# Sums of attention weights added by DMA transfers in the first six pairs, two more pairs masked on VectorE, three weight tiles

## The chip, the cores and the metric

The kernel runs on one core of a Trainium2 chip. The metric is the device time of one execution in microseconds (us). Before the change it is 1156.86 us, the median of three runs (1155.38 to 1157.08). The profiled execution has a span of 1152.4 us, at a mean granted TensorE clock of 0.995.

The engines are named as the profile names them: PE is TensorE's matmul, PEld its weight load, DVE is VectorE, ACT is ScalarE, POOL is GpSimd and SP is SyncE.

## The reference

Two blocks follow each other. The first is attention in which a query sees only the keys of its own hash bucket; the bucket is the sign pattern of six projections:

```python
q_bits = (einsum('bhsd,dk->bhsk', q, proj) > 0);  k_bits = (einsum(... k, proj) > 0)
mask = (sum(q_bits * 2**i))[:, :, :, None] == (sum(k_bits * 2**i))[:, :, None, :]
scores = where(mask, q @ k.T / sqrt(D), -1e9)
attn = exp(scores - max);  attn = attn / (sum(attn, axis=-1) + 1e-09)
x = (attn @ v) -> (B, S, H*D)
```

with 4 batches, 8 heads, 768 positions and a head size of 64. The second block mixes `x` by a Fourier transform over positions and channels, normalises the sum of `x` and the mixed values, and runs an MLP of 512 to 2048 to 512 with a residual:

```python
u = x + real(fft(fft(x, axis=1), axis=2))
out = u + relu(layernorm(u) @ w_ch1) @ w_ch2
```

All is float32; the two weight matrices come in a 64-bit form and are narrowed in the kernel.

## The kernel before

**Pairs of heads.** Attention works on 16 pairs of heads, `n` from 0 to 15, four in each batch: `attention(0)` runs pairs 0 to 3, `attention(1)` pairs 4 to 7, and so on. A pair goes through six steps `c`, one for each 128 keys. In a step, `weigh` (lines 796 to 829) multiplies keys by queries on PE (line 815), takes the exponential on ACT (line 819) into a weight tile `pk` of 128 keys by 2 query halves by 2 heads by 384 queries, and masks it. The tiles `pk` are shared by all pairs in turn; there are `NPK = 2` of them. Each has a 385th column with a small constant, which `values` (line 836) uses on PE when it multiplies the weights by the values.

**Two ways to mask.** For pairs in `LITE` (0 to 4), `prepare` makes sign bits of queries and keys (lines 735 to 742), and line 808 adds a large bias to the scores of pairs that match, by additional matmuls ahead of line 815; the exponential then does the masking. For all other pairs, `prepare` packs the bits into bucket numbers (lines 750 to 778: `bits`, `bt`, `qb`, `kb`), and DVE multiplies the weights by the comparison of bucket numbers, one instruction for each head (line 825). In a LITE pair after pair 0, all copies of transposed queries and keys go to ACT (line 531); in others every second one goes to DVE (line 529).

**The sums.** The denominator is the sum of the weights over all keys. DVE adds the six weight tiles of a pair into `acc` (line 898): the first addition takes tiles 0 and 1, then come four more. In `attention(0)` an addition is cut into two halves, later it is one instruction. At the end of a pair, `scale` (lines 841 to 869) lets PE sum `acc` over partitions by a matmul with ones (line 853), and DVE turns the result into reciprocals and multiplies the pair's output by them (lines 845 to 869).

**The order.** Within the block from line 1393 on, the order of PE, DVE, ACT and POOL is the order in which the program is written (a manual schedule); it covers `attention(0)`. In it, step by step, one slice of the first MLP matrix is narrowed: DVE lines 603 to 612 and ACT lines 611 to 616, while POOL issues the fetch of a later slice (line 657). In the first half of the columns, after every fourth slice PE takes the mean of its columns (line 623) and DVE subtracts it (line 631, centring). Each engine takes its instructions in order. `values` of a step and `scale` of a pair are issued one step later than the weights, so that a pair's sums stand on PE behind the scores of the next pair's step 0. In pair 3, two halves of a `fold` (lines 948 to 966), the first part of the Fourier mix, are put in as well.

From `attention(1)` on, a scheduler orders the work by its own costs; the Fourier mix and the MLP of batch b-1 run interleaved with the attention of batch b, and the second MLP matrix is narrowed during pairs 4 and 5.

Of the kernel before, what the change touches and what calls it, by code (L numbers as in the profile page):

```python
# [11 lines left out]
F32 = mybir.dt.float32  # L12
# [5 lines left out]
ALU = mybir.AluOpType  # L18
AX = mybir.AxisListType

P = 128
B, H, S, D = 4, 8, 768, 64
# [3 lines left out]
NT = S // P  # L26
NPAIR = H // 2
HALF = S // 2
# [451 lines left out]
def _main(  # L480
# [13 lines left out]
    nc = tc.nc  # L494
# [13 lines left out]
    def wt(shape, dtype, tag, name, bufs=2):  # L508
        return work.tile(shape, dtype, tag=tag, name=name, bufs=bufs)
# [4 lines left out]
    def pt(shape, name):  # L514

        turn[0] += 1
        if roomy[0] and turn[0] % 2:
            if turn[0] % 4 == 1:
                return ps_o.tile(shape, F32, tag="o", name=name)
            return ps_sc.tile(shape, F32, tag="sc", name=name)  # L520
        return ps_1.tile(shape, F32, tag="ps", name=name)
# [14 lines left out]
    def load(n, names="qkv", second=nc.sync):  # L536
        b, t = divmod(n, NPAIR)
        for nm in names:
            src = {"q": q, "k": k, "v": v}[nm]
            tag, bufs = ("vn", 2) if nm == "v" else ("qkn", 2)  # L540
            tl = wt([P, NT, 2, D], F32, tag, f"{nm}n{n}", bufs)
            for h in range(2):
                (second if h else nc.sync).dma_start(
                    tl[:, :, h, :], src[b, 2 * t + h].rearrange("(p c) d -> p c d", c=NT)
                )
            nat[nm, n] = tl
# [7 lines left out]
    make_identity(nc, ident)  # L554


    LITE = (0, 1, 2, 3, 4)
    pjw = const.tile([P, P], F32, tag="pjw", name="pjw")
    nc.gpsimd.memset(pjw, 0.0)
    for h in range(2):  # L560
# [8 lines left out]
    pw = const.tile([P, 2, P], BF16, tag="pw", name="pw")  # L569
    ones = const.tile([P, D], F32, tag="ones", name="ones")  # L570
# [3 lines left out]
    norms = const.tile([P, 2, NPAIR * B], F32, tag="norms", name="norms")  # L574


    NPK = 2
    pks = []
    for i in range(NPK):
        pk = const.tile([P, 2, 2, HALF + 1], F32, tag=f"pk{i}", name=f"pk{i}")  # L580
# [39 lines left out]
    def average(f):  # L620
        ps = pt([P, WC], f"wm{f}")
        for c in range(NDC):
            nc.tensor.matmul(
                ps, mean, w1[:, c, f : f + WC], start=(c == 0), stop=(c == NDC - 1)
            )
        return ps
# [68 lines left out]
    def prepare(n):  # L695

        lite = n in LITE
        act = lite and n > 0  # L700
# [89 lines left out]
    @contextmanager  # L790
    def behind():

        with tc.issue_after(last[0].ins), tc.high_priority(offset=AHEAD):
            yield

    def weigh(n, c):
# [3 lines left out]
        heads = [slice(h * D, (h + 1) * D) for h in range(2)]  # L800
        pk = pks[npk[0] % NPK]
        npk[0] += 1
# [28 lines left out]
    def values(n, c, pk, oos):  # L831

        for g in range(2):
            w = HALF + 1 - g
            for h in range(2):
                nc.tensor.matmul(  # L836
                    oos[g][h * D : (h + 1) * D, 0:w], nat["v", n][:, c, h, :],
                    pk[:, g, h, 0:w], start=(c == 0), stop=(c == NT - 1),
                )

    def scale(n, oos, acc):

        x = xs[n // NPAIR][:, n % NPAIR]
        vs = wt([P, 1], F32, "vs", f"vs{n}")
        nc.vector.tensor_copy(vs, oos[0][:, HALF : HALF + 1])
        halves = [x[:, g * HALF : (g + 1) * HALF] for g in range(2)]
        for g, xg in enumerate(halves):
            nc.scalar.activation(xg, oos[g][:, 0:HALF], AF.Identity, bias=vs)
        for g, xg in enumerate(halves):

            ps = pt([P, HALF], f"sum{n}_{g}")
            for h in range(2):
                nc.tensor.matmul(
                    ps[h * D : (h + 1) * D, :], ones, acc[:, g, h],
                    start=True, stop=True,
                )

            rt = wt([P, HALF], F32, "rt", f"rt{n}_{g}", 1)
            nc.vector.transpose(rt, ps)  # L859
            rc = wt([P, HALF // 32], F32, "rc", f"rc{n}_{g}")  # L860
            nc.vector.tensor_scalar(rc, rt[:, 0:HALF:32], S * EPS, None, op0=ALU.add)
            nc.vector.reciprocal(rc, rc)
            rb = wt([P, HALF], F32, "rb", f"rb{n}_{g}", 1)
            nc.vector.tensor_copy(
                rt.rearrange("p (j i) -> p j i", i=32),
                rc[:, :, None].broadcast_to([P, HALF // 32, 32]),
            )
            nc.vector.transpose(rb, rt)
            nc.vector.tensor_tensor(xg, xg, rb, op=ALU.mult)

    def attention(b):
        xs[b] = wt([P, NPAIR, S], F32, "x", f"x{b}")
        pending = []

        def finish():
            n, c, pk, oos, acc = pending.pop(0)
            with behind() if n >= NPAIR and t is not None else nullcontext():
                values(n, c, pk, oos)
            if c == NT - 1:
                scale(n, oos, acc)  # L880

        for t in range(NPAIR):
            n = NPAIR * b + t
            half = fold(b, 0) if t == NPAIR - 1 else iter(())
            if 1 < n + 1 < NPAIR * B:
                load(n + 1)
            ahead = prepare(n + 1) if n + 1 < NPAIR * B else iter(())
            oos = [ps_o.tile([P, 512], F32, tag="o", name=f"oo{n}_{g}") for g in range(2)]
            acc = wt([P, 2, 2, HALF], F32, "t6", f"acc{n}", 2)
            first = None  # L890
            for c in range(NT):
                new = weigh(n, c)
                if c == 0:
                    first = new[:, :, :, 0:HALF]
                else:

                    for g in (0, 1) if b == 0 else (slice(0, 2),):
                        nc.vector.tensor_tensor(  # L898
                            acc[:, g], (first if c == 1 else acc)[:, g],
                            new[:, g, :, 0:HALF], op=ALU.add,  # L900
                        )
                while pending:
                    finish()
                pending.append((n, c, new, oos, acc))
                if c > 2:
                    next(half, None)
                if c > 0:
                    next(ahead, None)
                yield
        t = None  # L910
        while pending:
            finish()
# [25 lines left out]
    def fold(b, cp):  # L938

        x = xs[b]
        if cp == 0:
            zs[b] = wt([P, 2, 2, 2, HALF], F32, "z", f"z{b}", 1)
        for pc in range(2):
            ef = wt([P, 2, S], F32, "t6", f"ef{b}_{cp}_{pc}", 2)
            e = ef[:, 0]
            nc.vector.tensor_tensor(
                e, x[:, cp], x[:, cp + 2], op=ALU.subtract if pc else ALU.add
            )  # L950
            f = ef[:, 1].rearrange("p (r n) -> p r n", r=2)
            for par in range(2):
                nc.vector.tensor_tensor(
                    f[:, par], e[:, 0:HALF], e[:, HALF:S],
                    op=ALU.subtract if par else ALU.add,
                )
            z = zs[b][:, cp, pc]
            n = HALF // 4 - 1
            for at, op in ((0, ALU.add), (2 * n + 3, ALU.subtract)):

                for i, first, last in ((0, 1, n), (n, 2 * n + 2, n + 1)):
                    nc.vector.tensor_tensor(
                        z[:, :, at + i : at + i + last], f[:, :, first : first + last],
                        turned(f, 2 * n + 1 if i == 0 else HALF - 1, last), op=op,
                    )
            nc.vector.tensor_copy(
                z[:, :, 2 * n + 1 : 2 * n + 3], f[:, :, 0 : n + 2 : n + 1]
            )
            yield
# [417 lines left out]
    next(other)  # L1387
    nc.sync.dma_start(ch, cn["ch"].ap())
    nc.sync.dma_start(sq, cn["sq"].ap())


    ET = mybir.EngineType
    with tc.manual_schedule(engines={ET.PE, ET.DVE, ET.Activation, ET.Pool}):
        for _ in prepare(0):
            pass
        roomy[0] = False
        for i, _ in enumerate(attention(0)):
            if i % 5 < 4:
                next(other, None)
        for _ in other:  # L1400
            pass
        pwf = wt([P, 2, P], F32, "t6", "pwf", 2)
        nc.sync.dma_start(pwf, cn["pw"].ap())
        nc.scalar.copy(pw, pwf)
        means = []
        for f in range(DFF // 2, DFF, WC):
            means.append((f, wt([P, WC], F32, "u", f"mean{f}", 2)))
            nc.scalar.copy(means[-1][1], average(f))
    for b in range(B):
# [17 lines left out]
        if b == B - 1:  # L1427
# [6 lines left out]
            ps = pt([1, 3, P], "norms_t")  # L1434
# [65 lines left out]
```

## Time and profile before

| | us | read as |
|---|---|---|
| median of three runs | 1156.86 | the time to beat |
| span of the profiled execution | 1152.4 | first to last instruction |
| PE busy | 1100.6 (96%) | ends of matmuls are modelled |
| DVE busy | 779.9 (68%) | |
| ACT busy | 451.8 (39%) | |
| POOL busy | 74.5 (6%) | issues DMA transfers, few operations |
| DMA moved | 103.11 MB | 89 GB/s over the span |

The page of the profile has the busy shares, the same as tenths in 40 slices of 28.8 us, and groups of like instructions. A row of a group names line, engine, operation, output and inputs with shape, count, the busy time, the mean of one in ns, and after the second bar the idle time of the engine just ahead of these instructions with what ended most of it. A row of a DMA group gives the size of one transfer and the median time from its issue to its landing. The table of windows gives, for a stretch of time, how long each engine was busy in it (with the number of instructions), the granted clock and the mean share of the DMA engines.

In this trace, attention(0) runs from about 12.5 us (the first scores on PE) to 130.6 us; pair 4 ends at 188.5 us and pair 5 at 267 us.

### The profile page before, as it was taken

Reading aid. Unit: us, or ns where it says so; the run is one execution under the profiler, and the core shown is the slowest. Engines: PE = TensorE matmul, PEld = TensorE weight load, DVE = VectorE, ACT = ScalarE, POOL = GpSimd, SP = SyncE. Lnnn points to the kernel's source line nnn. Section 1 sums busy time; section 2 is a strip of 40 time slices with the busy share of each in tenths; the row PEclk is TensorE's granted clock in tenths of the full one; section 3 lists DMA queues with packets and bytes.
Section 4 is the critical chain, followed back from the end, with each engine's and each line's share of the span. In section 5 each row is a group of like instructions: output and inputs, shape, how many; then the busy total and the mean of one; then the engine's idle time right before and its main releaser. Section 6 shows DMA issues by size and latency. Waiting matters only on the chain. (4 is left out here: it accounts for less than half of the span.)

```text
span 1152.4 us, 13749 instructions
## 1 busy us (share of the span) xinstructions
PE 1100.6 (96%) x4921; PEld 641.9 (56%) x4921; DVE 779.9 (68%) x1373; ACT 451.8 (39%) x858; POOL 74.5 (6%) x149
## 2 busy tenths in 40 slices
PE   7989889889999999999999999999999999999996
PEld 4444355444445445644674467654575468768675
DVE  4889959837938455883857877785775877644352
ACT  6778348623222212345224531345424431340420
POOL 1000001100100010020000002002000002010002
PEclk9999999999999999999999999999999999999998
DMA  9534135514611014113042315013104204131401
GB/s 272 151 80 121 40 93 168 167 44 146 224 48 47 17 32 152 28 51 106 15 151 68 86 52 177 15 42 96 47 31 139 64 28 164 48 96 56 154 24 39
DMA packets 131661, 103.11 MB, mean 89 GB/s; under 512 B 81280, under 2 KB 120320, under 8 KB 131584
## 3 DMA queue, kind: packets, MB, share of 16 engines
q1 hardware_dynamic: 123984, 82.35, 24.5%
q0 software_dynamic: 6032, 19.40, 5.1%
q8 instruction: 41, 0.67, 0.2%
q10 hardware_dynamic: 1568, 0.39, 0.2%
q14 instruction: 36, 0.29, 0.1%
HBM read 81.14 MB, written 20.97 MB: 89 GB/s over the span
## 5 line engine op out<-in xcount | busy, mean ns | idle before, releaser
L1214 PE MATMUL o<-w,h 128*128 128x256 f32 x864 | 194.0, 381 | 0.0
L819 ACT ACTIVATE pk<-sc 128x768 f32<-128x768 f32 x192 | 147.8, 808 | 101.2 <-PE sc L815 81.6
L1214 PEld LDWEIGHTS o<-w,h 128*128 128x128 f32 x864 | 162.3, 190 | 30.2 <-issue 3.4
L825 DVE SCALAR_TENSOR_TENSOR pk<-qb,kb,pk 128x768 f32<-128x768 bf16 x132 | 129.3, 1013 | 38.6 <-ACT pk L819 38.5
L815 PE MATMUL sc<-qt,kt 64*128 64x384 f32 x768 | 152.9, 501 | 0.9 <-ACT pk L819 0.9
L836 PE MATMUL oo<-pk,vn 128*64 128x385 f32 (+1 forms) x768 | 149.3, 498 | 1.8 <-DVE pk L825 1.8
L1314 PE MATMUL h_p<-x,w 128*128 128x384 f32 x384 | 140.2, 494 | 2.1 <-ACT qt L531 0.6
L898 DVE TENSOR_TENSOR acc<-acc,pk 128x1536 f32<-128x1536 f32 (+1 forms) x80 | 113.3, 1433 | 9.8 <-ACT pk L819 8.9
L1314 PE MATMUL h_p<-w 128*128 128x384 f32 x288 | 106.3, 492 | 2.9 <-ACT qt L531 1.8
L1314 PEld LDWEIGHTS h_p<-x,w 128*128 128x128 f32 x384 | 69.7, 190 | 56.5 <-ACT h L1346 3.4
L836 PEld LDWEIGHTS oo<-pk,vn 128*64 128x64 f32 x768 | 47.8, 136 | 90.5 <-issue 73.0
L1083 PE MATMUL h<-x,w 128*128 128x384 f32 x256 | 88.6, 499 | 4.1 <-DVE h L1089 3.1
L815 PEld LDWEIGHTS sc<-qt,kt 64*128 64x128 f32 x768 | 66.8, 186 | 44.7 <-issue 23.2
L1065 PE MATMUL o<-w,h 128*128 128x512 f32 x192 | 85.2, 596 | 0.6 <-DVE rt L859 0.6
L1314 PEld LDWEIGHTS h_p<-w 128*128 128x128 f32 x288 | 53.1, 190 | 43.4 <-ACT qt L531 2.4
L1083 PEld LDWEIGHTS h<-x,w 128*128 128x128 f32 x256 | 48.1, 193 | 40.6 <-issue 5.0
L1065 PEld LDWEIGHTS o<-w,h 128*128 128x128 f32 x192 | 35.5, 190 | 43.8 <-issue 41.7
L926 POOL DMA_DIRECT2D out_dram<-w x30 | 16.5, 552 | 468.7 <-issue 426.6
L1226 DVE SCALAR_TENSOR_TENSOR w<-o,rs,w 128x256 f32<-128x256 f32 x42 | 20.1, 481 | 32.2 <-PE o L1214 32.2
L1244 ACT COPY w<-o 128x256 f32<-128x256 f32 x18 | 6.7, 372 | 81.7 <-PE o L1214 81.7
L988 PE MATMUL cs<-ch,z 128*128 128x128 f32 (+3 forms) x192 | 31.8, 316 | 4.7 <-ACT kt L531 2.6
L1214 PE MATMUL o<-w 128*128 128x256 f32 x144 | 34.6, 383 | 1.2 <-DVE u L1226 0.9
(159 smaller groups left out, 1320.3 us busy)
## 6 DMA issues: line engine op xcount, KB each, us to landing
w<-ad SPq DMA_DIRECT2D x168, 128.0 KB, 2.0
w<-bd SPq DMA_DIRECT2D x42, 512.0 KB, 4.4
zraw<-in_moe_w_ch_dram POOLq DMA_DIRECT2D x21, 512.0 KB, 4.1
vn<-in_v_dram SPq DMA_DIRECT2D x32, 192.0 KB, 3.3
qn<-in_q_dram SPq DMA_DIRECT2D x31, 192.0 KB, 3.3
kn<-in_k_dram SPq DMA_DIRECT2D x31, 192.0 KB, 3.3
ad<-st SPq DMA_DIRECT2D x8, 512.0 KB, 3.7
bd<-st SPq DMA_DIRECT2D x8, 512.0 KB, 3.5
```

Of the source, the lines that this page charges most:

```text
L815: last[0] = nc.tensor.matmul(ps[:, h, 0:HALF], kt[rows, ks], qt[rows, qs], start=kb is not None, stop=True,)
L819: nc.scalar.activation(pk[:, g, :, 0:HALF], ps[:, :, 0:HALF], AF.Exp, scale=SCALE)
L825: nc.vector.scalar_tensor_tensor(w, qb[:, h].rearrange("p (g s) -> p g s", g=2), kb[:, h, c : c + 1], w, op0=ALU.is_equal, op1=ALU.mult,)
L836: nc.tensor.matmul(oos[g][h * D : (h + 1) * D, 0:w], nat["v", n][:, c, h, :], pk[:, g, h, 0:w], start=(c == 0), stop=(c == NT - 1),)
L898: nc.vector.tensor_tensor(acc[:, g], (first if c == 1 else acc)[:, g], new[:, g, :, 0:HALF], op=ALU.add,)
L926: nc.gpsimd.dma_start(out[b, s0 : s0 + 2 * w - 1 : 2, cols], src[at : at + w, cols])
L988: nc.tensor.matmul(ps[:, pc + 2 * lo : pc + 2 * hi - 1 : 2], z[:, cp, pc, par, t * P : (t + 1) * P], ch[:, cp, pc, lo:hi], start=(cp == 0) ...
L1065: nc.tensor.matmul(ps, hr, w2[:, fc, cols], start=(i == 0), stop=(i == len(rows) - 1))
L1083: nc.tensor.matmul(ps, w1[:, c, fc * P : (fc + 1) * P], x[:, c, g * HALF : (g + 1) * HALF], start=(c == 0), stop=(c == NDC - 1),)
L1214: nc.tensor.matmul(ps, a[:, r], right7[i][:, r], start=start and r == 0, stop=r == HF // 2 - 1, skip_group_check=not start,)
L1226: nc.vector.scalar_tensor_tensor(t[:, cols], src, r, t[:, cols], op0=ALU.mult, op1=ALU.add)
L1314: nc.tensor.matmul(ps, ring[n % NR][:, k], right[i][:, k], start=start and k == 0, stop=k == 1, skip_group_check=not start,)
```

## The change

In pairs 0 to 5 (`QUEUED`), the additions of steps 2, 3 and 4 leave DVE. Instead POOL issues a DMA transfer that reads a weight tile and adds it to `acc`. The additions of steps 1 and 5 stay on DVE. To make the transfer one run of bytes for each partition, `acc` gets the 385th column too. Pairs 2 and 3 leave `LITE`, so that DVE masks them and PE doesn't. A third weight tile lets a transfer read one tile while the next two are filled. As pair 2 needs the constant `pw` for its bucket numbers, this is loaded and converted early instead of after attention(0).

```diff
-    LITE = (0, 1, 2, 3, 4)
+    LITE = (0, 1, 4)
+
+    QUEUED = range(6)
...
-    NPK = 2
+    NPK = 3
...
-                    ps[h * D : (h + 1) * D, :], ones, acc[:, g, h],
+                    ps[h * D : (h + 1) * D, :], ones, acc[:, g, h, 0:HALF],
...
-            acc = wt([P, 2, 2, HALF], F32, "t6", f"acc{n}", 2)
+            acc = wt([P, 2, 2, HALF + 1], F32, "t6", f"acc{n}", 2)
...
                 if c == 0:
-                    first = new[:, :, :, 0:HALF]
+                    first = new
+                elif n in QUEUED and 1 < c < NT - 1:
+                    nc.gpsimd.dma_start(acc, new, accum_op=ALU.add)
                 else:
...
-                            acc[:, g], (first if c == 1 else acc)[:, g],
-                            new[:, g, :, 0:HALF], op=ALU.add,
+                            acc[:, g], (first if c == 1 else acc)[:, g], new[:, g],
+                            op=ALU.add,
                         )
...
+    pwf = wt([P, 2, P], F32, "u", "pwf", 2)
+    nc.sync.dma_start(pwf, cn["pw"].ap())
...
         for i, _ in enumerate(attention(0)):
+            if i == 0:
+                nc.scalar.copy(pw, pwf)
...
-        pwf = wt([P, 2, P], F32, "t6", "pwf", 2)
-        nc.sync.dma_start(pwf, cn["pw"].ap())
-        nc.scalar.copy(pw, pwf)
```

## The prediction

> **What bounds the kernel now.** The busy shares come first. TensorE (PE) is busy for 1100.6 of 1152.4 us, so a change pays only where PE stands still or loses work. The 40 slices (28.8 us each) tell where that is:
>
> ```profile
> PE   7989889889999999999999999999999999999996
> DVE  4889959837938455883857877785775877644352
> DMA  9534135514611014113042315013104204131401
> ```
>
> From the tenth slice on PE is at 9 nearly throughout; ahead of it lies attention(0), where PE stands at 8 or 9 and VectorE (DVE) too. I cut that stretch by pairs with the table of windows. The bounds are the times at which a pair's sums reach PE (line 853); the four pairs of attention(0) come first, then pairs 4 and 5.
>
> ```profile
> core 0: us, PE busy (x) PEld busy (x) DVE busy (x) ACT busy (x) POOL busy (x), PEclk, DMA share, GB/s
> 12.50:43.90 31.40, 30.46 (x170) 13.80 (x172) 23.30 (x39) 24.44 (x44) 2.62 (x5) 1.00 0.79 249
> 43.90:75.40 31.50, 28.86 (x160) 12.98 (x160) 26.83 (x48) 23.95 (x44) 2.35 (x5) 1.00 0.44 122
> 75.40:101.90 26.50, 25.25 (x151) 11.26 (x152) 25.09 (x45) 23.92 (x44) 0.00 (x0) 1.00 0.33 85
> 101.90:130.60 28.70, 24.08 (x139) 10.48 (x137) 25.42 (x53) 16.74 (x32) 0.11 (x1) 1.00 0.39 97
> 130.60:188.50 57.90, 53.53 (x296) 29.72 (x295) 42.70 (x78) 29.09 (x54) 3.69 (x7) 1.00 0.33 99
> 188.50:267.00 78.50, 70.51 (x263) 35.82 (x262) 50.21 (x84) 38.91 (x73) 4.77 (x9) 0.98 0.32 100
> ```
>
> Pair 0 is PE's (30.46 of 31.40). Pair 2 has two engines full at once: PE 25.25 and DVE 25.09 of 26.50. Whatever takes work from PE there and gives it to DVE makes DVE the bound. Pairs 4 and 5 leave PE 4.4 and 8.0 us of idle time. The groups give the prices:
>
> ```profile
> L825 DVE SCALAR_TENSOR_TENSOR pk<-qb,kb,pk 128x768 f32<-128x768 bf16 x132 | 129.3, 1013 | 38.6 <-ACT pk L819 38.5
> L898 DVE TENSOR_TENSOR acc<-acc,pk 128x1536 f32<-128x1536 f32 (+1 forms) x80 | 113.3, 1433 | 9.8 <-ACT pk L819 8.9
> L808 PE MATMUL sc<-qkb 64*128 64x384 bf16 x120 | 20.8, 327 | 5.5 <-ACT pk L819 5.1
> ...
> zraw<-in_moe_w_ch_dram POOLq DMA_DIRECT2D x21, 512.0 KB, 4.1
> ```
>
> A mask costs 1.01 us; in the timeline of DVE two in a row take 1.94. The second row mixes forms: in attention(0) an addition is two halves, 1.82 us together in the timeline; from pair 4 on it is one of 1.75.
>
> **What the Trainium skill says.** "DMA: Bandwidth & Descriptors", Anatomy of one DMA, prices a transfer issued from GpSimd at 2.0 us plus its bytes over 436 GB/s. That gives 3.2 us for 512 KB; the row above shows 4.1 us, so the price is rather low here. "Collectives: The Full Stack", The bandwidth ceiling, says that a sum in the DMA path is slowed because "the add needs **two source reads**". No addition by DMA is in the trace of before. The DMA page's Rules for kernel authors say that an accumulating transfer must wait for the semaphore of an earlier one on the same bytes; the changed program has these waits, so the three transfers of a pair run one after another.
>
> **The change part by part.**
> Removed from DVE: additions c = 2, 3, 4 of six pairs, 3 x 1.82 = 5.5 us in each of pairs 0 to 3, 3 x 1.75 = 5.3 us in pairs 4 and 5.
> Removed from PE (pairs 2 and 3 leave LITE): in the timeline a masking matmul pair of line 808 delays the next by 0.17 us, 12 x 0.17 = 2.0 us per pair; the bits take 0.8 + 0.5 + 0.2 us (lines 750, 764, 774) instead of 3.1 (line 735), 1.6 less. Together 7.2 us.
> Added to DVE: 12 masks in each of pairs 2 and 3, 6 x 1.94 = 11.6 us per pair. Preparing a masked pair takes 3.0 us (two qt copies 0.8, kt 0.55, bt 0.55, qb 0.95, kb 0.18) against 2.8 for a LITE one. ScalarE (ACT) loses 1.3 us of copies and gets one of 0.8 per pair.
>
> So DVE ends nearly even over attention(0): -22 + 23 + 0.4 us. But its order is written out by hand, and the load moves from pairs 0 and 1 into 2 and 3. From one scale() to the next, DVE's order in the changed program holds:
> - pair 1: scale 5.3, five weight slices of 1.9 (9.5), centring 2.5, preparing 3.0, two additions 3.6, the first mask of pair 2 1.9: 25.8 us.
> - pair 2: scale 5.3, five slices 9.5, six steps of masks 11.6, preparing 3.0, additions 3.6: 33.0 us.
> - pair 3: scale 5.3, one slice 1.9, five steps of masks 9.7, additions 3.6, half a fold 6.4, bits of pair 4 2.8: 29.7 us.
> Before, scale() began at 43.80, 75.74, 101.95 and 129.55 us (line 845 in the timeline). Pairs 2 and 3 together took 53.8 us and now need at least 62.7: **+8.9 us**, with PE waiting. Pair 1 is bound by ACT and PE; its 31.9 us lose 1.6 of PE work, 0.5 of ACT and 1.1 of PE's wait for qkb: 28.9.
>
> The added waits. DVE's addition c = 5 waits for the last transfer of its pair, and behind it on DVE's queue stand weight slices, masks or centring, then scale(); PE's sums wait for that addition, and all of the next pair's matmuls stand behind the sums. One transfer adds 788 KB. Nearest bounds: 3.8 us (the page's price, bytes once), 5.6 us (bytes twice, for two reads), and 9.1 us from the trace alone (128 KB took 2.0, 512 KB 4.1; that slope carried to 1,540 KB). I take 4.7, midway between the first two: the DMA engines' bytes go twice, but reads and writes overlap. Then:
> - pair 0: c = 2 is weighed at 28.6 us. The DMA engines are still full with weights (share 0.79), so 2 us more for the first: 35.3, 40.0, 44.7; addition to 46.5; centring and a slice behind it 4.4: scale(0) at 50.9, **+7.1**.
> - pair 1: c = 2 is ready 9.5 us after scale(0); + 14.1 + 1.8 + 3.8 (slice and mask behind it) = 29.2: 80.1 us.
> - pair 2: c = 2 is masked 15.6 us after; + 14.1 + 1.8 + 3.8 = 35.3: 115.4.
> - pair 3: 12.9 + 14.1 + 1.8 = 28.8, below DVE's own 29.7: 145.1, against 129.55: +15.5 us.
>
> After that, relief: PE's 12.4 us of idle time in pairs 4 and 5 stand partly behind DVE (1.4 us for qt, whose copy on DVE stood behind an addition; single waits for masks) and partly behind weight transfers (DVE waits 3.5 us for zraw). I take half, -6.2. The third weight tile frees ScalarE's exponentials from the last reader but one: at most the 4.9 us that PE waited for pk in attention(0), worth nothing where DVE binds. Loading pw earlier: one 128 KB transfer (2.0 us) and 0.4 us of ACT in pair 0, where ACT has 7 us free: nothing. Columns of 385 instead of 384: nothing. Sum: +15.5 - 6.2 = **+9.3 us, 1166 us**.
>
> **The rivals.**
> 1. The additions are quick (3.8 us): by the same steps 48.2, 77.1, 110.1, 139.8; +10.3 - 6.2: 1161.
> 2. They cost two full reads (5.6 us): 53.6, 85.5, 123.5, 155.0; +25.5 - 6: 1176. At 9.1 us: 64.1, 106.5, 155, 197, or 1218. For: the quoted sentence, and loads that land later than priced. Against: both operands lie in SBUF, not in HBM.
> 3. Faster: transfers hide, pair 1 shrinks to PE's own 26.5 us (scale(3) at 43.8 + 26.5 + 62.7 = 133.0, +3.5), and pairs 4 and 5 give back all 12.4: -8.9, 1148; with two thirds of it 1152. For: the windows show DVE full in 185 to 205 us, so 5.3 us less there may go through whole. Against: pairs 2 and 3 have more DVE work than time.
> 4. The two sides cancel: 1157.
>
> **How the numbers follow.** Transfers between 3.8 and 5.6 us with DVE binding: 0.54 (1161 to 1176, likeliest 1166). Slower transfers: 0.14. Faster: 0.25. No change: 0.07. Slower is thus 0.68. The range from 1148 to 1186 reaches from rival 3 to somewhat beyond 5.6 us; some 0.07 lies below it and 0.12 above.
>
> **What would show it.** After: DVE at 9 throughout pairs 2 and 3, with the distance of scale(1) to scale(3) 62 us or more; DVE waiting at the additions' second group for a DMA, and PE's sums for acc; the adding transfers landing in 4 to 6 us; pairs 4 and 5 shorter. Wrong if the transfers land under 4 us and pairs 0 and 1 shrink, or if scale(3) comes before 134 us.

## The result: 1221.6 us, 5.7% slower, and the profile after

The changed kernel takes 1221.63 us, the median of four runs (1219.56 to 1225.16), against 1156.12 us for the kernel before on the same chip. The ratio is 1.057, with an interval of 1.054 to 1.060. The forecast said slower, but 1166 us, and its range ended at 1186 us: the direction was right and the loss was seven times as large as forecast.

The slices of the changed kernel's page, each 30.6 us long, show where it is lost:

```profile
PE   4876678897999999999999999989999999999996
DVE  1366587395396755489485778779486778545352
PEclk8879799998999999999999999999999999999998
DMA  8754753658064111411304231411303121331501
```

From the eleventh slice on TensorE (PE) is nearly as full as before. In the first eight it is not, and neither is VectorE (DVE), which the forecast wanted to see at 9 throughout pairs 2 and 3 (slices 4 to 7: it shows 6, 5, 8, 7). An engine that has too much work is full; these two wait. The row of the granted clock holds 7 and 8 where it held 9 before.

The windows of the changed kernel run from one scale() to the next; the columns are the stretch, its length, the busy time of the five engines with their instructions, the granted clock, the DMA share and the rate:

```profile
core 0: us, PE busy (x) PEld busy (x) DVE busy (x) ACT busy (x) POOL busy (x), PEclk, DMA share, GB/s
12.50:68.00 55.50, 34.38 (x172) 14.40 (x172) 18.50 (x31) 24.82 (x45) 5.17 (x8) 0.80 0.74 194
68.00:110.90 42.90, 33.86 (x170) 13.81 (x168) 24.28 (x46) 23.80 (x42) 5.23 (x8) 0.86 0.64 145
110.90:155.60 44.70, 29.91 (x136) 11.06 (x134) 31.06 (x52) 23.95 (x42) 2.61 (x3) 0.81 0.52 106
155.60:191.90 36.30, 26.63 (x120) 10.28 (x116) 28.52 (x53) 16.82 (x31) 2.72 (x4) 0.95 0.58 124
191.90:248.40 56.50, 50.29 (x254) 28.49 (x253) 32.96 (x69) 24.78 (x46) 5.27 (x8) 0.91 0.50 121
248.40:332.60 84.20, 74.61 (x288) 38.79 (x288) 49.60 (x89) 41.05 (x78) 8.54 (x14) 0.94 0.49 136
```

scale() begins at 68.0, 110.9, 155.6 and 191.9 us. Against the kernel before it is 24.2, 35.1, 53.6 and 62.4 us late; pairs 4 and 5, from scale() to scale(), add only 3.0 and 2.0 us, so nearly all the loss is in attention(0). In no window is VectorE busy for more than four fifths of the time. VectorE's 31.1 us in pair 2 are close to the 33.0 us that the prediction summed up for it; the stretch lasts 44.7.

What VectorE and TensorE wait for stands in the groups and in the list of DMA issues (three rows of groups: busy time and mean ns, then idle time and its main releaser; one issue row: count, KB, median us to landing):

```profile
L827 DVE SCALAR_TENSOR_TENSOR pk<-qb,kb,pk 128x768 f32<-128x768 bf16 x156 | 152.4, 1013 | 41.0 <-ACT pk L821 41.0
...
L901 DVE TENSOR_TENSOR acc<-acc,pk 128x1540 f32<-128x1540 f32 (+1 forms) x50 | 81.2, 1630 | 31.2 <-DMA acc<-pk 29.9
...
L855 PE MATMUL sum<-acc,ones 128*64 128x384 f32 x128 | 28.8, 551 | 19.9 <-DVE acc L901 18.2
...
acc<-pk POOLq DMA_DIRECT2D x18, 770.0 KB, 6.8
```

The 24 more masks are there at their old price (x156, 1013 ns) and 30 additions are gone (x50). But VectorE idles 29.9 us in front of additions until an adding transfer has landed, and TensorE 18.2 us in front of the sums until that addition is made. A transfer takes 6.8 us (5.7 to 8.4), not 4.7. In the kernel before, the sums waited 2.4 us for additions:

```profile
L853 PE MATMUL sum<-acc,ones 128*64 128x384 f32 x128 | 25.3, 492 | 2.4 <-DVE acc L898 2.4
```

Two more rows come from the list of waits over the first 300 us (total, times, longest):

```profile
ACT qt L531 <- DVE qt L529: 18.4, 5, 6.6
...
ACT pw L1404 <- DMA pwf<-k_pw: 13.6, 1, 13.6
```

In the first row it is the place that is new, not the sum: the same list of the kernel before has

```profile
ACT qt L531 <- DVE qt L529: 21.0, 7, 6.6
```

but after the first few us these waits all lie behind attention(0), from 147.9 us on. Two of the changed kernel's, 4.6 and 6.6 us, lie in pairs 1 and 2.

The second row is a single wait, and the timelines of ScalarE and TensorE show what it does (start, length, and in brackets the idle time before and its releaser):

```profile
29.22 0.41 ACT L1404 CAST pw<-pwf 128x256 bf16<-128x256 f32 x1 [13.58 <-DMA pwf<-k_pw]
```

```profile
32.57 0.50 PE L810 MATMUL sc<-qkb 64*128 64x384 bf16 x2 [13.64 <-ACT pk L821]
32.84 1.51 PE L817 MATMUL sc<-qt,kt 64*128 64x384 f32 x4
```

The narrowing of pw stands in ScalarE's queue in front of the exponentials of step 1. Its load was issued behind ch, sq and the first weight slices, while the DMA engines were nearly full (a share of 0.89 from its issue at 19.6 us to its landing at 29.2). How long loads take there stood in the list of DMA issues of the kernel before:

```profile
sq<-k_sq SPq DMA_DIRECT2D x1, 770.0 KB, 15.8
ch<-k_ch SPq DMA_DIRECT2D x1, 512.0 KB, 13.5
```

For 13.6 us ScalarE does nothing; TensorE stops too, in front of scores that it can't make before ScalarE has taken an exponential. When TensorE starts again, four scoring matmuls take 1.51 us; in pair 0 of the kernel before they took 0.81:

```profile
18.60 0.81 PE L815 MATMUL sc<-qt,kt 64*128 64x384 f32 x4
```

The Trainium skill, "TensorE: Matmul & The Clock Gate", Part 1, says that TensorE's clock falls to half after an idle window of some 3.4 us and comes back after as long at work. The 1.51 us after a wait of 13.64 us agree with that, and so does the end of it: at 38.27 us, 5.7 us after the restart, four scoring matmuls take 0.81 us again.

### The profile page after: what moved, and what is told of

The parts are those of the page before. It is cut to its first block, busy times and chain, and to the rows that moved or that the text cites. A ratio compares the mean times of both kernels' runs of the same rounds, so it can differ in the third digit from the quotient of the medians.

```text
span 1223.4 us, 13688 instructions
## 1 busy us (share of the span) xinstructions
PE 1119.7 (92%) x4893; PEld 647.1 (53%) x4893; DVE 772.7 (63%) x1367; ACT 451.7 (37%) x854; POOL 90.3 (7%) x168
## 2 busy tenths in 40 slices
DMA packets 134253, 117.30 MB, mean 96 GB/s; under 512 B 81568, under 2 KB 120608, under 8 KB 134176
## 5 line engine op out<-in xcount | busy, mean ns | idle before, releaser
L827 DVE SCALAR_TENSOR_TENSOR pk<-qb,kb,pk 128x768 f32<-128x768 bf16 x156 | 152.4, 1013 | 41.0 <-ACT pk L821 41.0
L817 PE MATMUL sc<-qt,kt 64*128 64x384 f32 x768 | 160.3, 528 | 3.6 <-ACT pk L821 2.8
L838 PE MATMUL oo<-pk,vn 128*64 128x385 f32 (+1 forms) x768 | 154.9, 511 | 7.6 <-DVE pk L827 6.5
L901 DVE TENSOR_TENSOR acc<-acc,pk 128x1540 f32<-128x1540 f32 (+1 forms) x50 | 81.2, 1630 | 31.2 <-DMA acc<-pk 29.9
L817 PEld LDWEIGHTS sc<-qt,kt 64*128 64x128 f32 x768 | 70.0, 196 | 58.0 <-issue 27.4
L1317 PEld LDWEIGHTS h_p<-w 128*128 128x128 f32 x288 | 53.3, 190 | 41.9 <-ACT qt L531 2.3
L1068 PEld LDWEIGHTS o<-w,h 128*128 128x128 f32 x192 | 35.5, 190 | 43.8 <-issue 41.7
L855 PE MATMUL sum<-acc,ones 128*64 128x384 f32 x128 | 28.8, 551 | 19.9 <-DVE acc L901 18.2
L850 ACT ACTIVATE x<-oo,vs 128x384 f32<-128x384 f32 x32 | 16.8, 576 | 63.6 <-DVE vs L847 63.0
## 6 DMA issues: line engine op xcount, KB each, us to landing
vn<-in_v_dram SPq DMA_DIRECT2D x32, 192.0 KB, 3.4
qn<-in_q_dram SPq DMA_DIRECT2D x31, 192.0 KB, 3.3
kn<-in_k_dram SPq DMA_DIRECT2D x31, 192.0 KB, 4.5
```

The lines of the kernel that those rows point to most:

```text
L817: last[0] = nc.tensor.matmul(ps[:, h, 0:HALF], kt[rows, ks], qt[rows, qs], start=kb is not None, stop=True,)
L827: nc.vector.scalar_tensor_tensor(w, qb[:, h].rearrange("p (g s) -> p g s", g=2), kb[:, h, c : c + 1], w, op0=ALU.is_equal, op1=ALU.mult,)
L838: nc.tensor.matmul(oos[g][h * D : (h + 1) * D, 0:w], nat["v", n][:, c, h, :], pk[:, g, h, 0:w], start=(c == 0), stop=(c == NT - 1),)
L855: nc.tensor.matmul(ps[h * D : (h + 1) * D, :], ones, acc[:, g, h, 0:HALF], start=True, stop=True,)
L901: nc.vector.tensor_tensor(acc[:, g], (first if c == 1 else acc)[:, g], new[:, g], op=ALU.add,)
L1068: nc.tensor.matmul(ps, hr, w2[:, fc, cols], start=(i == 0), stop=(i == len(rows) - 1))
```

## The experiments

Three explanations were set against each other. Theory A: waits add up, namely the transfers' chain, the wait for pw and the copies of q and k that ScalarE and VectorE share; TensorE's slow clock makes each longer. Rival C: the masks on VectorE carry the loss. Rival D: the transfers cost by crowding the loads of weights. Further rivals come with single runs. Each run is timed beside the kernel before, which took 1154.7 to 1155.5 us.

### Each part alone

**pw later.** The changed kernel with

```diff
-            if i == 0:
+            if i == 3:
                 nc.scalar.copy(pw, pwf)
```

> The changed kernel, with the narrowing of pw on ScalarE moved from step 0 to step 3 of pair 0; the load stays where it is. Theory A (the copy waits 13.58 us for its load at 29.22 us, in ScalarE's queue ahead of the exponentials of step 1, and TensorE cools meanwhile): the 13.6 us come back nearly whole, 1205 to 1210 us; scale(0) at about 54 us instead of 68. Rival B (the sums wait for the adding transfers anyway, which start when the vectors are there, so that the wait for pw is hidden beside them): less than 4 us come back, 1218 to 1222 us. By the prediction, which costed the early load at nothing: 1221 us.

1210.0 us, ratio 1.048 (1.045 to 1.050): 11.6 us come back, which just meets theory A's 1205 to 1210. scale(0) is at 56.3 us, not 54: the narrowing still waited 8.7 us for the load at its new place, and VectorE's last addition waited 9.6 us for a transfer.

**pw early, nothing else.** The kernel before with the load behind sq's and the narrowing after step 0:

```diff
+    pwf = wt([P, 2, P], F32, "u", "pwf", 2)
+    nc.sync.dma_start(pwf, cn["pw"].ap())
...
         for i, _ in enumerate(attention(0)):
+            if i == 0:
+                nc.scalar.copy(pw, pwf)
...
-        pwf = wt([P, 2, P], F32, "t6", "pwf", 2)
-        nc.sync.dma_start(pwf, cn["pw"].ap())
-        nc.scalar.copy(pw, pwf)
```

> The kernel before, with nothing changed but the load and narrowing of pw, which go where the changed kernel has them. Theory A: the same wait of 13 to 14 us in front of the exponentials of step 1, nothing later to hide it: 1169 to 1172 us. Rival B (the wait costs only together with the adding transfers): 1156 to 1160 us.

1169.6 us, ratio 1.012 (1.010 to 1.015): 14.2 us, as theory A has it. The wait measured 15.2 us, and scale(0) came 14.8 us later. A move that the prediction costed at nothing costs more than the whole loss that it forecast.

**The transfers alone.** The changed kernel with pw loaded and narrowed after attention(0), where the kernel before has it, and

```diff
-    LITE = (0, 1, 4)
+    LITE = (0, 1, 2, 3, 4)
```

> The kernel before with the adding transfers, the longer sums and the third weight tile, but with pairs 2 and 3 masked on TensorE and pw loaded late as before. Theory A (three transfers of some 6.8 us in a chain for each pair, and the sums, scale() and the next pair's buffers behind them): each of six pairs loses some 4 to 8 us, 1180 to 1200 us. Rival C (the masks on VectorE carry most of the loss, the transfers only relieve VectorE): 1150 to 1160 us. Rival D (the transfers cost by crowding the loads of w1 and w2): a loss too, but with VectorE waiting for zraw, not for acc.

1194.3 us, ratio 1.034 (1.032 to 1.036), within theory A's numbers, though the six pairs lose from 12.8 us (pair 0) down to 2.5 (pair 5) and not 4 to 8 each. The first four scale() are 12.8, 19.7, 29.5 and 34.3 us late although VectorE has less to do. In the waits over the first 300 us, VectorE stood 48.0 us before additions for transfers and 10.5 us for zraw, where it stood 7.0 us for zraw before. So rival D has a share, but a small one, and rival C's "1150 to 1160" is out. The transfers are felt on ScalarE too: it stood 9.6 us, in pairs 0 and 2, until a transfer had read its weight tile and the tile was free again, three tiles or not.

**The masks alone.** The changed kernel with pw narrowed at step 3 and

```diff
-    QUEUED = range(6)
+    QUEUED = ()
```

> The changed kernel without any adding transfer (all additions on VectorE) and with the narrowing of pw at step 3: what is left of the change are the masks of pairs 2 and 3 on VectorE and the third weight tile. Theory A: what the prediction's sum gave for VectorE in pairs 2 and 3, +8.9 us, and up to 6 us for copies of q and k that wait behind it: 1163 to 1172 us. Rival C: 1190 us or more. Rival E (the third tile and the lighter TensorE pay for it): 1150 to 1157 us.

1194.7 us, ratio 1.034 (1.032 to 1.036). Theory A's figure missed by over 20 us, and rival C's "1190 us or more" came true: the masks alone cost as much as the transfers alone, so neither carries the loss by itself. Theory A's figure failed for two reasons. It took over the prediction's +8.9 us, which had the additions c = 2, 3, 4 gone from VectorE; here they are back, 5.5 us in each pair. The prediction's sums then become 38.5 us for pair 2 and 35.2 for pair 3; the trace gives 41.9 and 36.2, where the kernel before took 26.2 and 27.6. And scale(0) was 5.9 us late, from a wait of 4.9 us that was left for pw. Here VectorE is the fullest engine in pairs 2 and 3, busy for 36.4 of 41.9 and 34.1 of 36.2 us. The two halves, +38.9 and +39.3 us alone, give +54.6 together (the run with pw later): the transfers do take load off VectorE, as they are meant to, but for more than it is worth.

The trace of this run also shows the third wait, in pair 1 on ScalarE's timeline:

```profile
59.58 0.69 ACT L531 COPY qt<-trq 128x192 f32<-128x192 f32 x2 [5.03 <-DVE qt L529]
```

With LITE, ScalarE makes all four copies of qt itself; in pair 1 of the kernel before it made them without a wait:

```profile
48.52 1.21 ACT L531 COPY qt<-trq 128x192 f32<-128x192 f32 x4
```

Without LITE the copies alternate, and VectorE's stand behind scale(), a weight slice and an addition. ScalarE waits in order, with step 1's exponentials behind it.

### What makes a transfer slow

**Plain copies.** The kernel with the transfers alone, and

```diff
-                    nc.gpsimd.dma_start(acc, new, accum_op=ALU.add)
+                    nc.gpsimd.dma_start(acc, new)
...
-                        nc.vector.tensor_tensor(
-                            acc[:, g], (first if c == 1 else acc)[:, g], new[:, g],
-                            op=ALU.add,
+                        nc.vector.scalar_tensor_tensor(
+                            acc[:, g], (first if c == 1 else acc)[:, g], 1.0, new[:, g],
+                            op0=ALU.max, op1=ALU.add,
                         )
```

> The kernel with the adding transfers alone (pairs 2 and 3 masked on TensorE, pw late), but the 18 transfers copy the weights into acc instead of adding them; VectorE's additions become max-with-1-then-add of the same size. Left out: the sums over c = 2, 3, 4. Theory A (a transfer takes 7.0 us because it adds: acc is read as well as written): a plain copy of 770 KB lands in 4 to 5 us, each of the four first pairs gets some 4 to 6 us back, 1168 to 1182 us. Rival F (770 KB from memory on the chip to memory on the chip take that long in any case, or queue behind loads): 6 to 7 us a copy, 1188 to 1196 us.

This kernel leaves out the sums over three of the six steps. 1160.2 us, ratio 1.004 (1.003 to 1.005), below even theory A's range: 34 us of the 39 are gone. Bytes (117.30 MB in both), queue, chain and waits on semaphores are the same, and VectorE's other form of addition takes as long as the old one (mean 1629 ns against 1630); only the addition in the transfer is gone, and GpSimd's issue takes 0.53 us instead of 0.87. The issue row of this run:

```profile
acc<-pk POOLq DMA_DIRECT2D x18, 770.0 KB, 4.4
```

4.4 us against 7.0 with addition. What crosses the pairs' limit is the chain of three: three medians make 13.2 us, which fit almost beside the work of three steps (VectorE still stands 22.6 us for transfers, 12.3 of them in pair 0), and 21.0, which do not (48.0).

**Half the bytes.** The changed kernel with pw narrowed in pair 1, and

```diff
-                    nc.gpsimd.dma_start(acc, new, accum_op=ALU.add)
+                    nc.gpsimd.dma_start(acc[:, 0], new[:, 0], accum_op=ALU.add)
+                    nc.vector.tensor_tensor(
+                        acc[:, 1], acc[:, 1], new[:, 1], op=ALU.add
+                    )
```

> The changed kernel with pw narrowed in pair 1, and only the first half of the rows (acc[:, 0], 385 KB) added by the transfers; VectorE adds the second half in three more additions of 0.95 us for each pair. Theory A (the time of an adding transfer goes with its bytes, and the chain of three is what the pairs wait for): a transfer takes 3.5 to 5 us, the waits for acc at the last addition nearly go, VectorE has 2.9 us more in each pair: 1180 to 1198 us against 1212 with whole transfers. Rival H (a fixed cost for each adding transfer): still 6 us or more, with more work on VectorE, 1212 us or more.

1190.3 us, ratio 1.031 (1.029 to 1.033), against 1212.0 with whole transfers. In its list of DMA issues:

```profile
acc<-pk POOLq DMA_DIRECT2D x18, 385.0 KB, 4.3
```

Half the bytes take 2.5 us less, so rival H, a fixed cost, is out. It is no way out: VectorE takes the other half back.

**With and without other loads.** These medians mix two things, and the traces of the runs above and below part them. An addition beside which no other transfer is in flight takes 5.7 us (at 223.6 us in the changed kernel; the quickest of each run with whole additions takes as long), half of it 3.9 us (at 152.4 us in the run with half the bytes), and a plain copy 3.5 us (at 192.0 us in the run with masks and plain copies, below). The windows of the first and the last, with the columns as above:

```profile
223.60:229.30 5.70, 4.67 (x30) 2.61 (x30) 2.29 (x4) 3.11 (x6) 0.87 (x1) 1.00 0.70 138
192.00:195.50 3.50, 3.50 (x26) 2.42 (x25) 1.14 (x2) 1.22 (x3) 0.53 (x1) 1.00 0.55 225
```

Length times DMA share, an estimate of the work of the DMA engines, gives 4.0 us for the addition and 1.9 us for the copy: twice as much for the same 770 KB. So a lone addition is at the 5.6 us that the prediction had for two full reads. The 1.1 us more of the median go with other loads: the slowest addition of the changed kernel, 8.4 us at 81.9 us, has loads of q, k and weights in flight beside it.

### pw, relief and the third tile

**pw in pair 1.** The changed kernel with `if i == 6` in place of `if i == 0`:

> The changed kernel with the narrowing of pw in pair 1 (step 0), when its load has long landed: what the change costs without any wait for pw. With the narrowing at step 3 of pair 0 it still waited 4.9 us or so for the load. Theory A (waits add up): another 4 to 6 us less than there, 1203 to 1207 us, and scale(0) to scale(3) near 50, 93, 138 and 173 us; the prediction's own steps with 6.8 us in place of 4.7 for a transfer give 57, 93, 134 and 169. Rival B (hidden beside the transfers): 1209 to 1211 us.

1212.0 us, ratio 1.048 (1.046 to 1.051). Theory A missed, and the time is next to rival B's 1209 to 1211: no gain over step 3. ScalarE no longer waits for pw, but scale(0) stays at 56.6 us. VectorE's timeline says why:

```profile
50.61 1.83 DVE L901 TENSOR_TENSOR acc<-acc,pk 128x770 f32<-128x770 f32 x2 [17.75 <-DMA acc<-pk]
```

Without the wait for pw, pair 0 ends at its transfers, which share the DMA engines with the first loads (6.7 to 11.6 us each). The run with the transfers alone has the same scale(0), 56.6 us. So pw costs 14.2 us in the kernel before and 9.6 us here.

**Transfers in pairs 4 and 5 alone, and the third tile alone.** The transfers' kernel with `QUEUED = (4, 5)`:

> The kernel before with a third weight tile, the longer sums and adding transfers in pairs 4 and 5 alone. The prediction's step (relief of VectorE in these pairs gives back 6.2 us of TensorE's idle time): about 1150 us. Theory A (no relief: what VectorE saves is lost again to zraw loads that stand behind the transfers on GpSimd, and to the wait for the last transfer; with the adding transfers in all six pairs these two lost 3.8 and 2.5 us): 1157 to 1164 us.

The kernel before with `NPK = 3`:

> The kernel before with a third weight tile and nothing else of the change. The prediction (nothing in pairs 0 to 3 waits for a weight tile, some TensorE and ScalarE waits in pairs 4 and 5 might go): 1150 to 1157 us. Rival G (the third tile moves other tiles in the memory or lets the exponentials run ahead in front of more urgent work): 1158 us or more.

The third tile alone gives 1151.1 us, ratio 0.996 (0.995 to 0.998): a small gain. The waits of TensorE for pk at line 808 (total, times, longest, in the kernel before)

```profile
PE sc L808 <- ACT pk L819: 5.1, 9, 1.2
```

fall to 3.1 us in 7 waits in it. With the transfers in pairs 4 and 5 as well it is 1154.1 us, ratio 0.999 (0.998 to 1.000). Both expectations for that run left the tile out; beside the tile alone, the transfers there cost 3 us. There is no relief: TensorE stands idle for 5.3 and 10.0 us in pairs 4 and 5, and for 4.3 and 8.6 us with the tile alone. Zraw's loads, behind the transfers on GpSimd, take 5.2 us where the tile alone has 4.0.

### What the shared copies cost

**Copies on ScalarE, adding transfers.** The changed kernel with pw narrowed in pair 1, and

```diff
-        act = lite and n > 0
+        act = n in (1, 2, 3, 4)
```

> The changed kernel with pw narrowed in pair 1, and with all copies of the turned q and k for pairs 1 to 4 on ScalarE, where the changed kernel shares those of pairs 2 and 3 with VectorE. ScalarE waits 6.6 us for VectorE's copy in pair 2 and some 4.6 in pair 1. Theory A (these late copies hold up the exponentials): about the sum of these waits less the copies' own 2 us for each pair, 1203 to 1208 us. Rival I (the pairs end at the adding transfers or at VectorE's work anyway): 1210 to 1214 us.

1203.8 us, ratio 1.042 (1.041 to 1.044), against 1212.0: 8.2 us, as theory A has it.

**Masks with plain copies.** The changed kernel with pw narrowed in pair 1 and the plain copies as above:

> The changed kernel with pw narrowed in pair 1 and with plain copies (4.4 us in the run with the transfers alone) in place of the adding transfers (6.9 us), VectorE's additions again as max-with-1-then-add. Left out: the sums over c = 2, 3, 4. It is the prediction's case: a transfer of about the 4.7 us that was assumed, no wait for pw. The prediction's steps without the relief of 6.2 us that did not come: 1172 us, less the 4.4 us that the third tile brings, 1168 us, with scale(0) to scale(3) at 50.9, 80.1, 115.4 and 145.1 us. Theory A (these steps hold, late copies on top): 1166 to 1178 us. Rival J (the prediction also had the cost of the masks on VectorE too low): 1183 us or more, with scale(2) later than 122 us.

The same sums are left out. 1182.2 us, ratio 1.023 (1.021 to 1.025), between theory A and rival J, whose other sign, scale(2) later than 122 us, is there. Copies took 4.0 us; scale() came at 51.1, 87.9, 125.3 and 156.7 us. Pair 0 is right to 0.2 us. Pair 1 takes 36.7 us where the prediction's steps have 29.2, and most of the miss arises there.

**The same with the copies on ScalarE:**

> As the run with masks and plain copies (1182.2 us; the sums over c = 2, 3, 4 again left out), with the copies of the turned q and k for pairs 1 to 4 on ScalarE alone. Theory A (the 10 us that the prediction's steps miss there are the shared copies that stand behind other work on VectorE): 1172 to 1176 us, with the distance from scale(0) to scale(1) back from 36.7 us to some 30 to 32. Rival J (the masks cost VectorE more than the prediction has): 1179 to 1183 us.

Here too the sums are left out. 1175.2 us, ratio 1.017 (1.016 to 1.019): 7.0 of the 10 us, mostly theory A's, and rival J's 1179 to 1183 is out, though pair 1 still takes 33.5 us and not 30 to 32. The windows of pairs 1 and 2, first with plain copies and the copies of q and k shared:

```profile
51.12:87.85 36.73, 31.11 (x170) 13.19 (x168) 23.98 (x45) 24.13 (x43) 4.02 (x8) 0.92 0.55 169
87.85:125.33 37.48, 27.79 (x134) 10.59 (x134) 31.07 (x51) 24.00 (x42) 1.58 (x3) 0.86 0.40 122
```

and with those copies on ScalarE:

```profile
51.66:85.17 33.51, 29.59 (x170) 12.57 (x168) 23.08 (x43) 24.79 (x46) 4.22 (x8) 0.97 0.61 185
85.17:119.34 34.17, 26.86 (x134) 10.81 (x134) 29.95 (x48) 24.65 (x45) 1.58 (x3) 0.90 0.46 138
```

Both stretches are 3.3 us shorter with the same TensorE instructions (x170, x134). TensorE's busy time falls by 1.5 and 0.9 us with the clock's rise from 0.92 and 0.86 to 0.97 and 0.90. Pair 3, whose clock falls from 0.94 to 0.90, takes 1.4 us longer; pairs 4 and 5 are some 2 us shorter together.

**Tile and copies on the kernel before**, `NPK = 3` and `act = 0 < n < 7`:

> The kernel before with a third weight tile (which alone gave 1151.1 us) and the copies for pairs 5 and 6 on ScalarE alone as well. ScalarE waits 18 to 21 us over pairs 4 to 7 for VectorE's copies of qt. If these waits reach TensorE, whose idle time in pairs 4 and 5 is 12.4 us: 1145 to 1149 us; if TensorE has other work ready: 1150 to 1152 us.

1150.5 us, ratio 0.996 (0.995 to 0.998), the same as the tile alone: in pairs 4 and 5 the waits for shared copies do not reach TensorE, as it was expected for the case that it has other work ready. These two versions are faster than both kernels, by 0.4% against the one before.

## Why the prediction was wrong, point by point

The runs form a ledger from the forecast to the measurement. Its last three lines are each the difference of two measured kernels; the rest line is what is left, with the third tile's gain of 4.4 us in it. The sizes hold for this order: without masks the additions cost 34 us more than copies, with them 29.8; pw costs 14.2 us in the kernel before and 9.6 here. The rest is seen in the traces: by scale(3) the kernel of 1175.2 us is 7.0 us behind the prediction's steps, 4.3 of them in pair 1 and 3.0 in pair 3.

| step | us | time after it |
|---|---|---|
| forecast | | 1166 |
| "relief −6.2" did not come | +6.2 | 1172 |
| rest, not parted by a run | +3.0 | 1175.2 |
| copies shared by ScalarE and VectorE | +7.0 | 1182.2 |
| transfers that add, instead of copies | +29.8 | 1212.0 |
| wait for pw in front of pair 0's exponentials | +9.6 | 1221.6 |

- **"I take 4.7, midway between the first two."** This is the term that failed most. The adding transfer took 6.8 us; a plain copy took 4.0 to 4.4. "Reads and writes overlap" was the reason for going below two full reads, and no run supports it: even a lone addition takes 5.7 us, at the bound of 5.6. What inside the transfer doubles the work no run shows. The second half of the error is that other loads were priced for the first transfer of pair 0 alone, with 2 us; that one took 11.6 us (pw narrowed in pair 1). The prediction's own steps with 6.8 us in place of 4.7 give 57, 93, 134 and 169 us for the first four scale(), 24 us more at the last. Without the wait for pw the trace shows 56.6, 99.8, 145.0 and 181.6, and with the copies of q and k on ScalarE as well 56.6, 96.9, 139.2 and 174.8. So the chain's mechanism was right. What is left there is in pair 1, 40.2 us for 35.5: its first transfer is issued 1.6 us after its weights, behind a weight fetch in GpSimd's queue, and takes 9.4 us beside that fetch and the loads of q and k.
- **The row for 9.1 us, "or 1218".** That it comes near 1221.6 us is luck: no transfer takes 9.1 us in the median, and the wait for pw and the copies made up the difference. The slope that is named there gives 9.7 us besides, not 9.1.
- **"Loading pw earlier … nothing."** A term that was put at nothing costs 9.6 us. The cost was looked for in the wrong place: the load is 2.0 us and ScalarE has 7 us free, but the narrowing is in ScalarE's in-order queue before the load can land. Its issue stood behind slices of 512 KB, ch and sq, and the trace of before already had 13.5 and 15.8 us for the last two. The prediction asked what is queued behind the added waits on VectorE, and not behind this one on ScalarE.
- **"Pair 1 is bound by ACT and PE; its 31.9 us lose …: 28.9."** It counted which copies go from ScalarE to VectorE and not the order: ScalarE's own qt copy waits 4.6 us in pair 1 and 6.6 us in pair 2 for VectorE's. "c = 2 is ready 9.5 us after scale(0)" fails with it: 13.6 us in the changed kernel. In the runs with these copies on ScalarE they are ready after 9.8 us, so the estimate of 9.5 was good for that case. The sharing is worth 7.0 to 8.2 us. (31.9 less the three terms named is 28.7, not 28.9; only the first rival's sum uses it, and stays 1161.)
- **"Relief."** Additions leave VectorE in pairs 4 and 5, but TensorE's idle time does not fall. The measured sign is the other way, +3 us, and "pairs 4 and 5 shorter" was not seen: they are 3.0 and 2.0 us longer.
- **DVE at 33.0 and 29.7 us in pairs 2 and 3.** Right as a sum: busy time is 31.1 and 28.5 us, and the masks alone, with the additions put back, gave 41.9 and 36.2 us for 38.5 and 35.2. But in the changed kernel it is not what binds, so "DVE at 9 throughout" was not seen. The distance from scale(1) to scale(3), 81 us, meets "62 us or more" for another reason.
- **"DVE waiting at the additions' second group for a DMA, and PE's sums for acc"** was seen: 29.9 and 18.2 us.
- **The clock** was in no term. The kernel with the transfers alone has TensorE's 4921 instructions of before, and its first line of busy time is

```profile
PE 1111.6 (93%) x4921; PEld 645.2 (54%) x4921; DVE 749.8 (63%) x1343; ACT 451.4 (38%) x858; POOL 90.5 (8%) x168
```

against 1100.6 us before: 11 us more for the same matmuls. They are part of the prices above and not a line of their own.

## What to carry to other kernels

Work moved from an engine to a DMA queue pays only if the longest chain of transfers, at the measured time of that very kind and beside the loads that are then in flight, fits beside the work that goes on meanwhile; here three dependent transfers of 4.4 us nearly did, and of 7.0 us did not. When an instruction with an early load moves forward, ask when its load lands among the loads issued before it, and what stands behind the instruction on its own engine. When two engines share the copies of one tile, ask what stands in front of the copy on the fuller one: here ScalarE waited 4.6 and 6.6 us for VectorE's.

## What the runs showed of the hardware

- With no other transfer in flight, 770 KB between the same tiles took 3.5 us as a copy and 5.7 us as an addition, and 385 KB added took 3.9 us. In the medians, beside other loads, it was 4.0 to 4.4, 6.7 to 7.0 and 4.3 us. The price in the Trainium skill, "DMA: Bandwidth & Descriptors", Anatomy of one DMA (2.0 us and the bytes over 436 GB/s), gives 3.8 us for the copy; as an estimate with the bytes taken twice it gives 5.6 and 3.8 us for the two additions, which agrees with the lone ones within 0.1 us.
- A lone addition kept the DMA engines at work for some 4.0 us, a lone copy of the same bytes for 1.9 us (estimates from length and DMA share).
- Issuing an adding transfer held GpSimd 0.87 us, a plain one 0.53 us.
- 128 KB (pw) that took 2.0 us in the kernel before, loaded after attention(0), took 9.6 us behind the first loads in the changed kernel, where no further load was issued until 32.1 us, 14.3 us where loads were issued on from 22 us (masks alone), and 18.1 us with adding transfers beside them (pw narrowed at step 3).
- A wait of 13.6 us on TensorE is followed by matmuls of nearly twice the duration (1.51 us for 0.81).
